# Attention steps placed in the middle of matmul groups, and x made with tokens on partitions for four of eight batches

## The chip, the cores and the metric

The kernel runs on one core of one Trainium2 chip. A core has a matrix engine (TensorE, PE in the profile, with PEld for its weight loads), three other compute engines (VectorE or DVE, ScalarE or ACT, GpSimd or POOL), a queue engine (SyncE or SP) that here only issues DMAs, and 16 DMA engines. TensorE writes into PSUM, which has eight banks of 128 partitions by 512 fp32 values. The metric is the device time of one execution in microseconds; lower is better.

## What is computed

Linear attention without softmax, an RMS norm over each head's 64 outputs, and then a bilinear feed-forward layer on the tokens.

```python
# q, k, v: (8 batches, 8 heads, 576 tokens, 64); g_norm: (64,)
kv = np.einsum('bhsd,bhse->bhde', k, v)
out = np.einsum('bhsd,bhde->bhse', q, kv)
rms = np.sqrt(np.mean(out * out, axis=-1, keepdims=True) + 1e-06)
attn = out / rms * g_norm
x = attn.transpose(0, 2, 1, 3).reshape(4608, 512)
# w_a, w_b: (512, 1536); w_out: (1536, 512)
result = ((x @ w_a) * (x @ w_b)) @ w_out
```

## The kernel before

**Tiles and stages.** The 4608 tokens are worked on in nine strips of 512 for the feed-forward layer, and in eight batches of 576 for the attention. Matrix operands are bf16. x is kept transposed, with its 512 features on partitions: four tiles `xt` of 128 features (two heads each, a "pair") by all 4608 tokens. A strip has 16 steps. Steps 0 to 11 are units (`ffn_ab`): eight matmuls of 512 columns, four with w_a (`part_a`), after which ACT copies the result to SBUF as bf16, and four with w_b (`part_b`), after which DVE multiplies the two into a tile `ab`. Steps 12 to 15 are outputs (`ffn_o`): twelve matmuls over the twelve `ab` tiles for 128 tokens, a copy to SBUF by DVE or ACT in turn, and a store.

**Banks.** Units rotate over banks 0, 1 and 2: unit n writes its two halves into banks 2n mod 3 and 2n+1 mod 3. So the first half of unit n uses the bank that DVE's multiply of unit n-2 frees. Outputs take bank 3 and, every second time, the next bank of the rotation. The attention steps use banks 4 and 5 for x, 6 and 7 for the sums of squares, and 7 for kv.

**Attention within the strips.** While strip s runs (1 to 6), batch s+1 is made: `slot(A, s, n)` is called after step n and issues what is due there. `kv` is 40 small matmuls and two copies into `kvb`, a block-diagonal tile of a pair's two 64x64 matrices. `x` of pair p is two matmuls of 288 columns that give x transposed; `psq` squares them on ACT; `pss` sums the squares over each head's 64 partitions by two matmuls with a block matrix of ones, followed by the reciprocal root on ACT; `pst` multiplies x by the root and by g on DVE, into `xt`. Before the change, kv is at step 5 in strips 1 and 2 and at step 2 later; x of the four pairs is at steps 7, 9, 11, 13 (4, 7, 10, 12 later), and pss and pst one step after each.

**Order.** There is no scheduler: each engine runs its instructions in the order in which the code issues them, with waits where one instruction needs another's result or its buffer. This holds for the DMA queues too. SP carries the stores of the outputs and the transposes of q (`transpose_q`, from a DRAM copy `qs` of a batch's q into `qT`). POOL carries the loads of later batches (`load_late`). `load_late(b)` starts with a one-element copy into `gate` that reads q's transposed tile of batch b-1 and so waits for its transpose, and then issues six DMAs (two for `qs`, two each for k and v). In strips from 2 on, `transpose_q(b+1)` and `load_late(b+2)` are issued after step 8.

**Start and end.** Batches 0 and 1 are made in other ways at the start, and are not touched by the change except for the name of `xt`. Strips 7 and 8 have no attention.

Of the kernel before, what the change touches and what calls it, by code (L numbers as in the profile page):

```python
# [8 lines left out]
FP32 = mybir.dt.float32  # L9
BF16 = mybir.dt.bfloat16  # L10
AF = mybir.ActivationFunctionType
# [4 lines left out]
def kernel(  # L16
# [11 lines left out]
    nc = tc.nc  # L28

    B, H, S, D = q.shape  # L30
    d_model = H * D
    n_tok = B * S
    d_ff = moe_w_a.shape[1]
    KC = d_model // 128
    FC = d_ff // 128
    NP = H // 2
    HF = S // 2
    STRIP = 512
# [2 lines left out]

    EC, EP = 6, 96
    EARLY = 2
    KORD = tuple(range(KC))

    pool = ctx.enter_context(tc.tile_pool(name="sb", bufs=1))
# [2 lines left out]
    def sb(shape, dt, name):  # L49
        return pool.tile(shape, dt, name=name, tag=name)  # L50
# [7 lines left out]

    kt = [sb([EP, H, EC, D], BF16, f"kt{i}") for i in range(EARLY)]
    vt = [sb([EP, H, EC, D], BF16, f"vt{i}") for i in range(EARLY)]  # L60

    LC = S // 128
    ktl = [sb([128, H, LC + 1, D], BF16, f"ktl{i}") for i in range(2)]
    vtl = [sb([128, H, LC + 1, D], BF16, f"vtl{i}") for i in range(2)]
    qt = [sb([EP, H, EC, D], BF16, f"qt{i}") for i in range(EARLY)]

# [1 line left out]
    kvs = [sb([128, NP, D], BF16, f"kvs{i}") for i in range(2)]  # L68

    kvb = [sb([128, NP, 128], BF16, f"kvb{i}") for i in range(2)]  # L70
    xt = [sb([128, n_tok], BF16, f"xt{i}") for i in range(KC)]
    abt = [[sb([128, STRIP], BF16, f"ab{i}_{f}") for f in range(FC)] for i in range(2)]
    a_sb = [sb([128, STRIP], BF16, f"asb{i}") for i in range(4)]
    sq = [sb([128, 2, HF], BF16, f"sq{i}") for i in range(3)]
    rs = [sb([128, 2, HF], FP32, f"rs{i}") for i in range(3)]
    o_sb = [sb([128, d_model], FP32, f"osb{i}") for i in range(4)]
    o_end = sb([128, d_model // 2], FP32, "o_end")
    ident = sb([128, 128], BF16, "ident")
# [3 lines left out]
    eps_t = sb([128, 1], FP32, "eps_t")  # L82
    warm = sb([128, 1], FP32, "warm")
    k32 = sb([EP, 2, EC, D], FP32, "k32")
    v32 = sb([EP, 2, EC, D], FP32, "v32")
    q32 = sb([EP, 2, EC, D], FP32, "q32")

    qc = sb([EP, EC, 2 * D], BF16, "qc")
    kc0 = sb([EP, EC, 2 * D], BF16, "kc0")
# [5 lines left out]
    P = psum.tile([128, 8, STRIP], FP32, name="P", tag="P")  # L95
    O = 3

    qs_d = {b: tc.dram_tile([S, d_model], BF16, name=f"qs{b}") for b in range(EARLY, B)}

# [23 lines left out]
    def load_late(b):  # L123
        if b > EARLY:

            nc.gpsimd.tensor_copy(gate, qT[(b - 1) % 2][0:1, 0, 0:1])  # L126
        d = qs_d[b].rearrange("t (h d) -> t h d", h=H)
        for hs in (slice(0, NP), slice(NP, H)):
            nc.gpsimd.dma_start(out=d[:, hs, :], in_=q[b, hs].rearrange("h t d -> t h d"))  # L129
        n = 128 * LC  # L130
        for t, src in ((ktl[b % 2], k), (vtl[b % 2], v)):
            nc.gpsimd.dma_start(
                out=t[:, :, 0:LC, :],
                in_=src[b, :, 0:n].rearrange("h (t c) d -> t h c d", c=LC),
            )
            nc.gpsimd.dma_start(
                out=t[0 : S - n, :, LC, :], in_=src[b, :, n:].rearrange("h t d -> t h d")
            )

    def transpose_q(b):  # L140
        nc.sync.dma_start_transpose(qT[b % 2], qs_d[b])


    class Attn:
# [5 lines left out]
        def kv(self, p, o):  # L150

            if self.b < EARLY:
                kk, vv, rows = kt[self.b], vt[self.b], [EP] * EC
# [66 lines left out]
        def pst(self, p, x0, hs=(0, 1)):  # L220
            for h in hs:
                t0 = self.b * S + h * HF
                nc.vector.scalar_tensor_tensor(  # L223
                    out=xt[p][:, t0 : t0 + HF],
                    in0=P[:, x0 + h, 0:HF],
                    scalar=g_col,
                    in1=rs[p % 3][:, h, :],
                    op0=ALU.mult,
                    op1=ALU.mult,
                )  # L230
# [10 lines left out]
                )  # L241


    class Unit:
        n = 0

# [5 lines left out]
        def mm(self, w, kcs):  # L252
            t0 = self.s * STRIP
            for kc in kcs:
                nc.tensor.matmul(  # L255
                    self.a if w is wa_t else self.b,
                    lhsT=w[:, kc, self.fc * 128 : (self.fc + 1) * 128],
                    rhs=xt[kc][:, t0 : t0 + STRIP],
                    start=(kc == KORD[0]),
                    stop=(kc == KORD[-1]),  # L260
                )
# [4 lines left out]

        def part_a(self, kcs=KORD):
            self.mm(wa_t, kcs)
            nc.scalar.copy(self.t, self.a)  # L269

        def part_b(self, kcs=KORD):
            self.mm(wb_t, kcs)
            nc.vector.tensor_mul(abt[self.s % 2][self.fc], self.b, self.t)  # L273

        def rest(self, kcs=KORD):
            self.part_a(kcs)
            self.part_b(kcs)

    n_ab = [0]

    def ffn_ab(s, fc):
        i = n_ab[0]
        n_ab[0] += 2
        Unit(s, fc, i % 3, (i + 1) % 3).rest()

    def store(t0, t, e0, e1, eng=nc.sync):
        i = 0
# [15 lines left out]
    def o_mm(s, g, i, fcs, e0=0, e1=d_model):  # L303
        for fc in fcs:
            nc.tensor.matmul(  # L305
                P[:, i, e0:e1],
                lhsT=abt[s % 2][fc][:, g * 128 : (g + 1) * 128],
                rhs=wo_t[:, fc, e0:e1],
                start=(fc == 0),
                stop=(fc == FC - 1),  # L310
            )

    def o_out(s, g, i):
        n = n_o[0]
        n_o[0] += 1
        t = o_sb[n % 4]
        if n % 2:
            nc.scalar.copy(t, P[:, i, :])  # L318
        else:
            nc.vector.tensor_copy(t, P[:, i, :])  # L320
        store(s * STRIP + g * 128, t, 0, d_model)

    def ffn_o(s, g, i=O):
        o_mm(s, g, i, range(FC))
        o_out(s, g, i)


# [41 lines left out]
    X, SS = (4, 0), 6  # L369


    A = Attn(0)
# [9 lines left out]
    t = P[:, 2, :].bitcast(BF16)[:, 0:S].rearrange("q (c t) -> q c t", c=EC)  # L382
# [4 lines left out]
    for c in range(EC):  # L387
        nc.tensor.matmul(
            P[:, SS, 0 : 2 * D],
            lhsT=kc0[:, c, :],  # L390
            rhs=vc[:, c, :],
            start=(c == 0),
            stop=(c == EC - 1),
# [10 lines left out]
    for p in range(1, NP):  # L404
        i = X[p % 2]
# [38 lines left out]
    for fc in range(4, FC):  # L444
        ffn_ab(0, fc)


    A = Attn(1)
    h1, h2 = range(0, FC // 2), range(FC // 2, FC)

    nc.sync.dma_start(out=gate_d, in_=vt[1][0:1, H - 1, EC - 1, D - 1 : D])
    ffn_o(0, 0, X[0])
    pieces = [(1, h1), (1, h2), (2, h1), (2, h2), (3, h1), (3, h2)]
    for n, (g, fcs) in enumerate(pieces):
# [24 lines left out]
    def slot(A, s, n):  # L479

        kb = P[:, 7, 0 : NP * D].rearrange("q (p e) -> q p e", e=D)
        k0, kn, xs = (5, 1, (7, 9, 11, 13)) if s < 3 else (2, 1, (4, 7, 10, 12))
        if k0 <= n < k0 + kn:
            for p in range((n - k0) * NP // kn, (n - k0 + 1) * NP // kn):
                A.kv(p, kb[:, p, :])
            if n == k0 + kn - 1:
                A.kv_out(slice(0, NP), kb)
        for p in range(NP):
            if n == xs[p]:
                A.x(p, X[0])  # L490
                A.psq(p, X[0])
            if n == xs[p] + 1:
                A.pss(p, SS)
                A.pst(p, X[0])

    for s in range(1, N_STRIP - 1):
        b = s + 1
        A = Attn(b) if b < B else None
        for n in range(FC + 4):
            if n >= FC:  # L500
                i = O if n % 2 == 0 else n_ab[0] % 3
                n_ab[0] += n % 2
                ffn_o(s, n - FC, i)
            elif s > 1 or n > 1:
                ffn_ab(s, n)
            if A:
                slot(A, s, n)
            if n == 8 and b + 1 < B:
                if s > 1:
                    transpose_q(b + 1)  # L510
                    if b + 2 < B:
                        load_late(b + 2)
                else:
                    load_late(3)
        if s == 1:
            transpose_q(3)
            load_late(4)
    last = N_STRIP - 1
    for fc in range(FC):
        ffn_ab(last, fc)  # L520
    for g in range(3):
        ffn_o(last, g, (O, 4)[g % 2])
# [38 lines left out]
```

## Time and profile before

| | |
|---|---|
| median of 8 runs | 322.63 us (322.34 to 323.46) |
| profiled execution | 322.58 us, of which the span from first to last instruction is 320.8 |
| granted TensorE clock | 1.000 |
| a strip (windows of TensorE's timeline, strips 4 and 5) | 33.9 us each |
| DVE and ACT busy in such a strip | 13.5 and 14.4 us |
| POOL's gate copies | 5, waiting 85.0 us in all |
| q transposes on SP | 6, 5.1 to 12.0 us from issue to landing |

A row of the groups names the line, the engine, the operation, what it writes and reads, its shape and count, then busy time in us and the mean of one in ns, then the idle time ahead of it and what ended it. A line of the timeline gives the start, the length, the engine, the line, the operation and the count, and in brackets the idle time before it. "POOL gate L126 <- DMA qT<-qs" in the waits means that the copy at L126 waited for that DMA, followed by total, number and longest. Matmuls are pipelined and their ends are modelled, so that the distance between starts tells more than the length.

### The profile page before, as it was taken

How to read it: one execution, taken by the hardware profiler on the slowest of the kernel's cores; microseconds unless marked ns; L12 is line 12 of the kernel's file. 1: busy time of each engine (PE TensorE's matmuls, PEld its weight loads, DVE VectorE, ACT ScalarE, POOL GpSimd, SP SyncE). 2: the span in 40 equal slices, each digit the busy share in tenths (PEclk: the TensorE clock that was granted, in tenths of full speed). 3: DMA queues.
4: the chain of work that ended last, by engine and by line, in shares of the span. 5: the costliest groups of instructions: out<-in, count | busy, mean ns of one | idle time of the engine just before them, and what ended most of it. 6: DMA issues, size and time to landing. Idle time of an engine off the chain costs nothing.

```text
span 320.8 us, 4732 instructions
## 1 busy us (share of the span) xinstructions
PE 315.2 (98%) x1883; PEld 150.7 (47%) x1883; DVE 124.8 (39%) x218; ACT 125.5 (39%) x217; POOL 70.3 (22%) x94
## 2 busy tenths in 40 slices
PE   8999999999999999999999999999999999999995
PEld 3444454444445444444444445444444444444443
DVE  4543344344234433453244423532354243313421
ACT  3643165353335423552355325432454233123310
POOL 8944990070034080160080000000000000000000
PEclk9999999999999999999999999999999999999999
DMA  8999999999369999999699151003000200020002
GB/s 180 197 196 200 197 181 232 138 95 158 88 90 150 144 117 209 101 125 163 141 72 151 65 116 25 0 35 99 0 2 0 98 35 0 24 90 21 0 33 98
DMA packets 79308, 32.60 MB, mean 102 GB/s; under 512 B 49974, under 2 KB 74806, under 8 KB 79286
## 3 DMA queue, kind: packets, MB, share of 16 engines
q0 software_dynamic: 59120, 18.44, 52.9%
q1 hardware_dynamic: 19810, 13.44, 17.9%
q10 hardware_dynamic: 356, 0.43, 0.4%
q8 instruction: 14, 0.23, 0.3%
q14 instruction: 8, 0.07, 0.1%
HBM read 37.75 MB, written 12.98 MB: 158 GB/s over the span
## 4 chain that ended last, share of the span: by engine, by line
PE 80%; DMA 13%; POOL 5%; issue 1%; ACT 0%; POOLq 0%
PE P L255 49%; PE P L305 26%; DMA wb_t<-in_moe_w_b_dram 5%; DMA vtl<-in_v_dram 5%; PE P L235 2%; PE P L209 2%; DMA kt<-in_k_dram 2%; DMA wo_t<-in_moe_w_out_dram 2%; PE P L158 1%; POOL qs L129 1%; POOL qt L106 1%; POOL wo_t L121 0%; POOL wa_t L360 0%; POOL wb_t L360 0%; POOL vt L106 0%
## 5 line engine op out<-in xcount | busy, mean ns | idle before, releaser
L273 DVE TENSOR_TENSOR ab<-P,asb 128x512 bf16<-128x512 f32 x108 | 74.5, 692 | 124.6 <-PE P L255 123.6
L255 PE MATMUL P<-xt,wa_t 128*128 128x512 bf16 x432 | 111.9, 379 | 0.0
L255 PE MATMUL P<-xt,wb_t 128*128 128x512 bf16 x432 | 111.7, 379 | 0.0
L305 PE MATMUL P<-wo_t,ab 128*128 128x512 bf16 (+1 forms) x444 | 97.9, 373 | 0.0
L269 ACT CAST asb<-P 128x512 bf16<-128x512 f32 x108 | 63.0, 585 | 81.8 <-PE P L255 80.3
L255 PEld LDWEIGHTS <-wb_t 128*128 128x128 bf16 x432 | 42.2, 98 | 50.9
L305 PEld LDWEIGHTS <-ab 128*128 128x128 bf16 x444 | 43.1, 98 | 45.6
L255 PEld LDWEIGHTS <-wa_t 128*128 128x128 bf16 x432 | 41.7, 98 | 44.8 <-issue 0.5
L223 DVE SCALAR_TENSOR_TENSOR xt<-P,g_col,rs 128x288 bf16<-128x288 f32 x64 | 30.1, 513 | 24.3 <-ACT rs L213 24.3
L213 ACT ACTIVATE rs<-P,eps_t 128x576 f32<-128x576 f32 (+1 forms) x33 | 23.9, 727 | 20.8 <-PE P L209 16.5
L318 ACT COPY osb<-P 128x512 f32<-128x512 f32 x17 | 10.0, 585 | 48.6 <-PE P L305 46.8
L205 ACT ACTIVATE sq<-P 128x576 bf16<-128x576 f32 x31 | 20.2, 650 | 20.6 <-PE P L235 18.3
L320 DVE COPY osb<-P 128x512 f32<-128x512 f32 x18 | 12.5, 692 | 32.4 <-PE P L305 32.3
L129 POOL DMA_DIRECT2D qs<-in_q_dram x12 | 19.6, 1636 | 2.2 <-issue 2.1
L126 POOL COPY gate<-qT 1x1 bf16<-1x1 bf16 x5 | 0.9, 176 | 85.0 <-DMA qT<-qs 85.0
L209 PE MATMUL P<-sq,ones 128*128 128x288 bf16 x64 | 13.2, 286 | 0.5 <-ACT sq L205 0.4
L235 PE MATMUL P<-qT,kvb 128*128 128x288 bf16 x56 | 11.9, 286 | 0.0
L169 ACT CAST kvb<-P 64x256 bf16<-64x256 f32 (+1 forms) x20 | 6.0, 301 | 11.8 <-PE P L158 11.7
L209 PEld LDWEIGHTS <-ones 128*128 128x128 bf16 x64 | 6.2, 98 | 7.4 <-issue 0.4
L330 PE MATMUL P<-zeros 128*128 128x512 bf16 x17 | 7.2, 569 | 1.2 <-DVE eps_t L345 1.2
L235 PEld LDWEIGHTS <-kvb 128*128 128x128 bf16 x56 | 5.5, 98 | 6.0
L121 POOL DMA_DIRECT2D wo_t<-in_moe_w_out_dram x12 | 6.4, 531 | 6.7 <-DMA wb_t<-in_moe_w_b_dram 3.3
(55 smaller groups left out, 83.5 us busy)
## 6 DMA issues: line engine op xcount, KB each, us to landing
out_dram<-osb SPq DMA_DIRECT2D x23, 256.0 KB, 2.0
qs<-in_q_dram POOLq DMA_DIRECT2D x12, 288.0 KB, 6.1
ktl<-in_k_dram POOLq DMA_DIRECT2D x6, 512.0 KB, 8.5
vtl<-in_v_dram POOLq DMA_DIRECT2D x6, 512.0 KB, 10.6
out_dram<-osb SPq DMA_DIRECT2D x13, 128.0 KB, 2.3
wo_t<-in_moe_w_out_dram POOLq DMA_DIRECT2D x12, 128.0 KB, 5.9
wa_t<-in_moe_w_a_dram POOLq DMA_DIRECT2D x5, 256.0 KB, 9.0
wb_t<-in_moe_w_b_dram POOLq DMA_DIRECT2D x5, 256.0 KB, 9.6
```

What stands on the lines that cost most here:

```text
L129: nc.gpsimd.dma_start(out=d[:, hs, :], in_=q[b, hs].rearrange("h t d -> t h d"))
L205: nc.scalar.activation(sq[p % 3], P[:, i0 : i0 + 2, 0:HF], AF.Square)
L209: nc.tensor.matmul(P[:, i0 + h, 0:HF], lhsT=ones, rhs=sq[p % 3][:, h, :], start=True, stop=True)
L213: nc.scalar.activation(rs[p % 3][:, h0:h1, :], P[:, i0 + h0 : i0 + h1, 0:HF], AF.Abs_reciprocal_sqrt, bias=eps_t,)
L223: nc.vector.scalar_tensor_tensor(out=xt[p][:, t0 : t0 + HF], in0=P[:, x0 + h, 0:HF], scalar=g_col, in1=rs[p % 3][:, h, :], op0=ALU.mult, o ...
L235: nc.tensor.matmul(P[:, i0 + h, 0:HF], lhsT=kvb[self.b % 2][:, p, :], rhs=self.qT[:, p, h * HF : (h + 1) * HF], start=True, stop=True,)
L255: nc.tensor.matmul(self.a if w is wa_t else self.b, lhsT=w[:, kc, self.fc * 128 : (self.fc + 1) * 128], rhs=xt[kc][:, t0 : t0 + STRIP], st ...
L269: nc.scalar.copy(self.t, self.a)
L273: nc.vector.tensor_mul(abt[self.s % 2][self.fc], self.b, self.t)
L305: nc.tensor.matmul(P[:, i, e0:e1], lhsT=abt[s % 2][fc][:, g * 128 : (g + 1) * 128], rhs=wo_t[:, fc, e0:e1], start=(fc == 0), stop=(fc == F ...
L318: nc.scalar.copy(t, P[:, i, :])
L320: nc.vector.tensor_copy(t, P[:, i, :])
```

## The change

Three things are changed.

First, `slot` may be called in the middle of a step too: between `part_a` and `part_b` of a unit and between the two halves of an output's twelve matmuls, with n less a half. For batches 2 and 3 (strips 1 and 2), kv goes from step 5 to 6, x of the pairs to 7, 9.5, 12 and 13.5, and pss with pst to 8, 10.5, 12.5 and 14.

Second, for batches 4 to 7 (strips 3 to 6), x is made with tokens on partitions. The 576 tokens are five chunks (four of 128, one of 64), and a chunk starts with every step from 3.5 on. `tx` is four matmuls of 128 columns with the chunk of q as weights and `kvb` as moving operand, into one of the banks 4, 5, 6, and a Square on ACT from PSUM into `sqt` (fp32). `tss`, half a step later, sums each head's 64 squares on DVE. `trs`, half a step later, takes the reciprocal root on ACT (8 values a token) and multiplies it with g on POOL into `sqt`, 512 values a token. `txt`, half a step later, multiplies that with x in PSUM on DVE, into a bf16 tile `x_tok` (three buffers, in the place of the first q tile), and SP issues a DMA transpose from there into `xt`. pss with its 288-column matmuls and pst fall away for these batches. The last multiply of chunk 4 is issued at step 8.5, its product at 9.

Third, `xt` becomes one tile with the four groups of features in its middle dimension, and g is loaded once more, onto all 128 partitions, by SP.

The lines that set the order of step 8 are not changed: `transpose_q(b+1)` and `load_late(b+2)` come after `slot(A, s, 8)`.

```diff
+    def tx(self, c, i):
+        t0 = c * 128
+        n = min(128, S - t0)
+        for p in range(NP):
+            nc.tensor.matmul(
+                P[0:n, i, p * 128 : (p + 1) * 128],
+                lhsT=self.qT[:, p, t0 : t0 + n],
+                rhs=kvb[self.b % 2][:, p, :], start=True, stop=True,
+            )
+        nc.scalar.activation(
+            sqt[c % 2][0:n], P[0:n, i, :].rearrange("t (h d) -> t h d", h=H), AF.Square
+        )
+    def tss(self, c):
+        n = min(128, S - c * 128)
+        nc.vector.reduce_sum(sst[c % 2][0:n], sqt[c % 2][0:n], axis=mybir.AxisListType.X)
+    def trs(self, c):
+        n = min(128, S - c * 128)
+        nc.scalar.activation(
+            rst[c % 2][0:n], sst[c % 2][0:n],
+            AF.Abs_reciprocal_sqrt, bias=eps_t[0:n], scale=1.0 / D,
+        )
+        nc.gpsimd.tensor_mul(
+            sqt[c % 2][0:n],
+            rst[c % 2][0:n].unsqueeze(2).to_broadcast([n, H, D]),
+            g_all[0:n].unsqueeze(1).to_broadcast([n, H, D]),
+        )
+    def txt(self, c, i):
+        t0 = c * 128
+        n = min(128, S - t0)
+        t = x_tok[:, c % 3]
+        nc.vector.tensor_mul(
+            t[0:n], P[0:n, i, :].rearrange("t (h d) -> t h d", h=H), sqt[c % 2][0:n]
+        )
+        t0 += self.b * S
+        nc.sync.dma_start_transpose(
+            xt[:, :, t0 : t0 + n], t[0:n].rearrange("t h d -> t (h d)")
+        )
...
-    def ffn_ab(s, fc):
+    def ffn_ab(s, fc, between=None):
         i = n_ab[0]
         n_ab[0] += 2
-        Unit(s, fc, i % 3, (i + 1) % 3).rest()
+        u = Unit(s, fc, i % 3, (i + 1) % 3)
+        u.part_a()
+        if between:
+            between()
+        u.part_b()
...
-    def ffn_o(s, g, i=O):
-        o_mm(s, g, i, range(FC))
+    def ffn_o(s, g, i=O, between=None):
+        o_mm(s, g, i, range(FC // 2))
+        if between:
+            between()
+        o_mm(s, g, i, range(FC // 2, FC))
         o_out(s, g, i)
...
     def slot(A, s, n):
-        k0, kn, xs = (5, 1, (7, 9, 11, 13)) if s < 3 else (2, 1, (4, 7, 10, 12))
...
+        if s < 3:
+            k0, xs, ss = 6, (7, 9.5, 12, 13.5), (8, 10.5, 12.5, 14)
+        else:
+            k0, xs, ss = 2, (4, 7, 10, 12), (5, 8, 11, 13)
+        if n == k0:
+            for p in range(NP):
+                A.kv(p, kb[:, p, :])
+            A.kv_out(slice(0, NP), kb)
+        if A.b >= BY_TOKEN:
+            for c in range(LC + 1):
+                d = n - (k0 + 1.5) - c
+                i = 4 + c % 3
+                if d == 0:
+                    A.tx(c, i)
+                elif d == 0.5:
+                    A.tss(c)
+                elif d == 1:
+                    A.trs(c)
+                elif d == 1.5:
+                    A.txt(c, i)
+            return
+        if n in xs:
+            p = xs.index(n)
+            A.x(p, X[0])
+            A.psq(p, X[0])
+        if n in ss:
+            p = ss.index(n)
+            A.pss(p, SS)
+            A.pst(p, X[0])
...
         for n in range(FC + 4):
+            amid = (lambda n=n: slot(A, s, n - 0.5)) if A else None
             if n >= FC:
                 i = O if n % 2 == 0 else n_ab[0] % 3
                 n_ab[0] += n % 2
-                ffn_o(s, n - FC, i)
+                ffn_o(s, n - FC, i, amid)
             elif s > 1 or n > 1:
-                ffn_ab(s, n)
+                ffn_ab(s, n, amid)
             if A:
                 slot(A, s, n)
             if n == 8 and b + 1 < B:
                 if s > 1:
                     transpose_q(b + 1)
                     if b + 2 < B:
                         load_late(b + 2)
```

More of the change, by code (lines that the diff above doesn't have):

```diff
@@ L43 @@
     EARLY = 2
+    BY_TOKEN = 4
     KORD = tuple(range(KC))
@@ L70 @@
     kvb = [sb([128, NP, 128], BF16, f"kvb{i}") for i in range(2)]
-    xt = [sb([128, n_tok], BF16, f"xt{i}") for i in range(KC)]
+    xt = sb([128, KC, n_tok], BF16, "xt")
     abt = [[sb([128, STRIP], BF16, f"ab{i}_{f}") for f in range(FC)] for i in range(2)]
@@ L75 @@
     rs = [sb([128, 2, HF], FP32, f"rs{i}") for i in range(3)]
+    sqt = [sb([128, H, D], FP32, f"sqt{i}") for i in range(2)]
+    sst = [sb([128, H], FP32, f"sst{i}") for i in range(2)]
+    rst = [sb([128, H], FP32, f"rst{i}") for i in range(2)]
+    g_all = sb([128, D], FP32, "g_all")
     o_sb = [sb([128, d_model], FP32, f"osb{i}") for i in range(4)]
@@ L85 @@
     v32 = sb([EP, 2, EC, D], FP32, "v32")
-    q32 = sb([EP, 2, EC, D], FP32, "q32")
+    q_x = sb([128, 2 * EC * D], FP32, "q_x")
+    q32 = q_x[0:EP].rearrange("p (h c d) -> p h c d", h=2, c=EC)
+    x_tok = q_x.bitcast(BF16).rearrange("p (c h d) -> p c h d", c=3, h=H)
     qc = sb([EP, EC, 2 * D], BF16, "qc")
@@ L223, in pst @@
                 nc.vector.scalar_tensor_tensor(
-                    out=xt[p][:, t0 : t0 + HF],
+                    out=xt[:, p, t0 : t0 + HF],
                     in0=P[:, x0 + h, 0:HF],
@@ L241, in x @@
                 )
+        def tx(self, c, i):
[5 more added lines that the diff above has]
+                    lhsT=self.qT[:, p, t0 : t0 + n],
+                    rhs=kvb[self.b % 2][:, p, :],
+                    start=True,
+                    stop=True,
+                )
[8 more added lines that the diff above has]
+            nc.scalar.activation(
+                rst[c % 2][0:n],
+                sst[c % 2][0:n],
+                AF.Abs_reciprocal_sqrt,
+                bias=eps_t[0:n],
+                scale=1.0 / D,
+            )
[15 more added lines that the diff above has]
+            )
     class Unit:
@@ L257, in mm @@
                     lhsT=w[:, kc, self.fc * 128 : (self.fc + 1) * 128],
-                    rhs=xt[kc][:, t0 : t0 + STRIP],
+                    rhs=xt[:, kc, t0 : t0 + STRIP],
                     start=(kc == KORD[0]),
@@ L445 @@
         ffn_ab(0, fc)
+    nc.sync.dma_start(out=g_all, in_=g_norm.partition_broadcast(128))
     A = Attn(1)
@@ L481, in slot @@
         kb = P[:, 7, 0 : NP * D].rearrange("q (p e) -> q p e", e=D)
-        k0, kn, xs = (5, 1, (7, 9, 11, 13)) if s < 3 else (2, 1, (4, 7, 10, 12))
-        if k0 <= n < k0 + kn:
-            for p in range((n - k0) * NP // kn, (n - k0 + 1) * NP // kn):
-                A.kv(p, kb[:, p, :])
[L486 to L494, printed above, removed]
+        if s < 3:
[4 more added lines that the diff above has]
+            for p in range(NP):
+                A.kv(p, kb[:, p, :])
+            A.kv_out(slice(0, NP), kb)
[20 more added lines that the diff above has]
+            A.pst(p, X[0])
     for s in range(1, N_STRIP - 1):
```

## The prediction

> **What bounds the kernel now.** I read the page first, then the table of groups, then TensorE's timeline strip by strip, then the timelines of POOL and of SP.
>
> From the page:
>
> ```profile
> PE 315.2 (98%) x1883; PEld 150.7 (47%) x1883; DVE 124.8 (39%) x218; ACT 125.5 (39%) x217; POOL 70.3 (22%) x94
> ...
> PE 80%; DMA 13%; POOL 5%; issue 1%; ACT 0%; POOLq 0%
> ```
>
> TensorE is busy almost throughout and carries the chain that ended last. So a TensorE instruction saved is time saved, and a TensorE stall is time lost, one for one.
>
> TensorE's timeline (start us, length, engine, line, operation, count, idle before it), pieces of four places:
>
> ```profile
> 7.28 0.50 PE L388 MATMUL P<-vc,kc 96*128 96x128 bf16 x6
> ...
> 61.06 0.32 PE L158 MATMUL P<-vtl,ktl 128*64 128x64 bf16 x8
> 61.91 0.69 PE L158 MATMUL P<-vtl,ktl 128*64 128x64 bf16 x32 [0.54 <-DMA vtl<-in_v_dram]
> ...
> 69.95 0.53 PE L235 MATMUL P<-qT,kvb 128*128 128x288 bf16 x2
> 70.31 1.02 PE L255 MATMUL P<-xt,wa_t 128*128 128x512 bf16 x4
> ...
> 162.99 0.41 PE L235 MATMUL P<-qT,kvb 128*128 128x288 bf16 x2
> 163.24 1.03 PE L255 MATMUL P<-xt,wa_t 128*128 128x512 bf16 x4
> 164.10 1.03 PE L255 MATMUL P<-xt,wb_t 128*128 128x512 bf16 x4
> ```
>
> Ends are modelled, so I price by the distance of starts. Four 512-column matmuls take 164.10 - 163.24 = 0.86 us, 0.216 each; a unit (eight) takes 1.73, an output (twelve) 2.59. Two 288-column ones take 163.24 - 162.99 = 0.25, about 0.12 each. At 69.95 the same pair takes 0.36: 0.12 us of waiting for the banks. Six 128-column matmuls start within 0.50 - 0.22 = 0.28 us, 0.057 each. In strip 1, kv waits 0.54 us for vtl. Strips 3 to 6 have no stall of TensorE.
>
> The two element-wise rows that free the units' banks (mean ns of one after the busy time):
>
> ```profile
> L273 DVE TENSOR_TENSOR ab<-P,asb 128x512 bf16<-128x512 f32 x108 | 74.5, 692 | 124.6 <-PE P L255 123.6
> ...
> L269 ACT CAST asb<-P 128x512 bf16<-128x512 f32 x108 | 63.0, 585 | 81.8 <-PE P L255 80.3
> ```
>
> POOL's timeline in strip 3, SP's timeline, and one line of the waits:
>
> ```profile
> 134.64 0.18 POOL L126 COPY gate<-qT 1x1 bf16<-1x1 bf16 x1 [14.21 <-DMA qT<-qs]
> 135.13 3.26 POOL L129 DMA_DIRECT2D qs<-in_q_dram  x2 [0.31 <-issue]
> 138.37 0.91 POOL L132 DMA_DIRECT2D ktl<-in_k_dram  x1
> 139.26 0.70 POOL L136 DMA_DIRECT2D ktl<-in_k_dram  x1
> 139.94 0.91 POOL L132 DMA_DIRECT2D vtl<-in_v_dram  x1
> 140.81 0.72 POOL L136 DMA_DIRECT2D vtl<-in_v_dram  x1
> ```
>
> ```profile
> 123.70 7.12 SPq L141 DMA_TRANSPOSE qT<-qs  x1
> ...
> 154.83 2.23 SPq L141 DMA_TRANSPOSE qT<-qs  x1
> ...
> 188.72 3.11 SPq L141 DMA_TRANSPOSE qT<-qs  x1
> ```
>
> ```profile
> POOL gate L126 <- DMA qT<-qs: 85.0, 5, 22.5
> ```
>
> POOL runs in order. The gate copy holds it until the transposed q has landed (22.5 us at the longest), and the six loads behind it occupy POOL from 134.64 to 141.53, 6.9 us. Before the change nobody waits for POOL there. From the transpose's issue at 154.83 to its gate (160.92 in the same timeline) it is 6.1 us; landings are 5.1 to 12.0 us, the long ones while loads run.
>
> **What the Trainium skill says.** "GPSIMD Engine Reference", section 3.1, gives 4497 ns for a two-input fp32 tensor_tensor of 2048 elements a lane, so 1.12 us for 512; with about 0.1 us of start (POOL's smallest memset, at L545, takes 0.10) I estimate 1.2 us. No trace of before has such an operation. "DMA: Bandwidth & Descriptors", section DMA Transpose (X-bar), says that transposes are issued from SP or ACT alone; here all six stand on SP, so the new ones share its queue with the stores and q's transpose. "TensorE: Matmul & The Clock Gate", Part 1, says that after an idle window of 3.4 us the array runs at half rate until it has been busy for such a window. The trace agrees at the start: the 512-column dummies follow each other at 0.43 us (weight loads at 4.16 and 4.59) until about 7 us, then at full rate. It shows no idle stretch later.
>
> **Part 1: batches 2 and 3, finer places.** Same instructions, other places. kv comes one unit later (1.73 us), which covers its 0.54 us wait. x now comes 1.5 steps after the last pss, at least 2.6 us, where the trace needs 104.08 + 0.12 - 102.11 = 2.1; four waits of 0.12 go. Gain 0.54 + 0.48 = 1.0 us. Pair 3 still ends at step 14, so strip 2's start is no later. If vtl should be later still, at most the 0.54 stays.
>
> **Part 2: batches 4 to 7, TensorE.** Out: 8 x and 8 pss, 16 x 0.12 = 1.96 us. In: 20 matmuls of 128 columns, 20 x 0.057 = 1.14. Gain 0.82 a batch, 3.3 over four. Both parts: 4.3.
>
> **Part 2: the loop of one chunk.** Each chunk passes ACT (Square, about 0.60 by L269), DVE (sum of 512 from SBUF, no such row: between the 0.56 of the cast of 768 from SBUF at L377 and the 0.69 of L273, I take 0.60), ACT (rsqrt of 8 columns, 0.21 by the 0.20 of the one-column activation at L347), POOL (1.2), DVE (product, 0.69 by L273). In DVE's queue they alternate: ab, product of c, sum of c+1, next ab. Product of c waits for POOL, POOL for rsqrt, rsqrt for the sum of c, and the sum of c stands behind the product of c-1. So one round is 0.60 + 0.21 + 1.2 + 0.69 + four handovers (0.17) = 2.87 us, while TensorE brings a unit with a chunk every 1.73 + 0.23 = 1.96. Counted from a strip's start (unit 4 ends at 9.83, after kv):
>
> - products end at 13.7, 16.6, 19.4, 22.3 for chunks 0 to 3;
> - ab of units 7, 8, 9 stand behind them: 17.9, 20.7, 23.6;
> - a unit's first half needs the bank that ab of two units before frees, so unit 10 starts at 20.8 and not 19.6, unit 11 waits for 23.6, and ends at 25.4. Without waits it ends at 22.8.
>
> Behind DVE's waiting product stand the ab and through them TensorE; behind ACT's waiting rsqrt the next Square and copy. Loss 2.5 us in each strip from 3 to 6. Bounds: with POOL at 0.8 us the round is 2.5 and the loss 1.1; at 2.0, 5.7. I see no reason for a gain here.
>
> **Part 2: chunk 4 behind the gate.** The queues' order in the changed program: on SP, x transposes of chunks 0 to 3, then q's transpose of batch b+1, then chunk 4's. On POOL, the multiplies of chunks 0 to 3, then gate and six loads of batch b+2, then the multiply of chunk 4. That holds in strips 3 and 4 (batches 4 and 5); in 5 and 6 there is no load. Before, q's transpose issued as soon as the previous strip's stores were out; now it comes after product 3: 22.3 + 0.6 (its x transpose, estimated from 2.23 us for 576 rows) = 22.9. Gate at +6.1 = 29.0 (the loads are over by then, so not the long landing), POOL free at +6.9 = 35.9, multiply to 37.1, product to 37.8, ab of unit 10 to 38.5, of 11 to 39.2. TensorE runs on through unit 11 and ten matmuls of the first output, to 27.5, and then has nothing: 11 us idle. The output ends at 39.5, against 25.4 without any wait: 14.1 us lost in each of the two strips (the 2.5 of the loop is within it). With POOL at 0.8 and a landing of 5.1 it is 11.2; with POOL at 2.0, 18.1.
>
> An idle of 11 us is more than three such windows, so TensorE comes back at half rate for 3.4 to 6.8 us: 1.7 to 3.4 us lost, I take 2.5, twice 5.0; at the low end 0, since no later stretch shows it.
>
> x itself is late for nobody: the next strip first needs chunks 0 and 1 at most, which are out by 17. The loads of b+2 come later, but have a strip to spare. The merge of x^T into one tile adds no wait within a strip. g's load of 128 rows is small and off the path.
>
> **Sum.** The profiled execution took 322.58 us (span 320.8 plus 1.8 around it), the median is 322.63. 322.6 - 4.3 + 2 x 14.1 + 2 x 2.5 + 5.0 = 356.5.
>
> **Rivals.**
> - B, the gate alone: POOL is quick (0.65 us), the loop costs 0.6 a strip, the gate 11.6. 318.3 + 24.4 + 5.0 = 347.7. For it: POOL's small operations are quick here. Against: none has two fp32 inputs of this size.
> - C, a slow loop: POOL needs 2.0 us with its broadcast operands. 318.3 + 2 x 18.1 + 2 x 5.7 + 5.0 = 370.9.
> - D, faster: TensorE has 5.6 us of other work after the place of the last product (two units and ten matmuls, 3.45 + 2.16). If q's transpose and the loads held POOL for less than that, and the multiply took under 0.5 us, all waits would be hidden and the saved matmuls alone counted: 318.3. It decides below 5.6 us; against it stand 5.1 (the quickest landing) + 6.9 measured.
> - The x transposes could themselves be late, so that strip 4's first unit waits for them; with twenty microseconds to spare I give that no time of its own.
>
> **How the numbers follow.** The likeliest case 0.60, B 0.19, C 0.12, D 0.06, all cancelling 0.03. Differences under 0.2% (0.65 us) can't be told from none here. Predicted 356.5. The low end is POOL at 0.8, landing 5.1, no cold clock: 318.3 + 2 x 11.2 + 2 x 1.1 = 342.9; the high end stops just short of C's centre. Range 343 to 370; it holds most of the first case, B, and a part of C. Faster 0.06, same 0.03, slower 0.91.
>
> **What would show it.** In strips 3 and 4, DVE's product of chunk 4 waits over 10 us for POOL, POOL's gate follows the q transpose that was issued after chunk 3's, and TensorE stands idle in the first output, then runs 512 columns at 0.43 us. In strips 5 and 6 the products are about 2.9 us apart and TensorE loses 2 to 3 us. Strips 1 and 2 have no stall in x or kv. I am wrong if TensorE has no idle stretch over 5 us in strip 3, or if the products keep pace with the units.

## The result

The changed kernel takes 353.35 us (median of 11 runs, 352.5 to 357.55) against 322.6 us before: a ratio of 1.097, with a 95% interval from 1.095 to 1.100. The profiled execution took 356.11 us, with a span of 354.3 us and a mean granted clock of 0.957. The forecast was 356.5 us, in a range of 343 to 370, and slower.

From the page of the kernel after (busy time by engine, the row of the granted clock in 40 slices of the span, and the chain that ended last):

```profile
PE 320.7 (91%) x1899; PEld 149.5 (42%) x1899; DVE 133.0 (38%) x226; ACT 117.1 (33%) x225; POOL 91.1 (26%) x114
...
PEclk9699999999999999957999959999999999999999
...
PE 78%; POOL 6%; DMA 5%; issue 4%; DVE 4%; ACT 1%; DVEq 0%; SPq 0%; POOLq 0%
```

TensorE's share of the span fell from 98% to 91%. DVE has come into the chain with 4%, and of POOL's share, 6% where it was 5%, half is now the new multiply (`sqt` at L282, 3% in the page's list by lines). The clock row has three dips that were not there before: one near the start and two in the middle.

I read the start of every strip's first unit from TensorE's timeline; the differences are the strips' lengths in us. The last two columns belong to experiments further down.

| strip | before | after | loads after chunk 4 | product later, g late |
|---|---|---|---|---|
| before strip 1 | 50.61 | 53.53 | 51.98 | 50.57 |
| 1 and 2 | 68.99 | 67.79 | 67.80 | 67.79 |
| 3 | 33.90 | 48.56 | 35.08 | 33.28 |
| 4 | 33.90 | 48.30 | 35.15 | 33.28 |
| 5 | 33.90 | 35.14 | 35.15 | 33.28 |
| 6 | 33.89 | 35.16 | 35.15 | 33.28 |

Of the 33.5 us by which the span grew, 29.1 are in strips 3 and 4, 2.5 in strips 5 and 6, and 2.9 ahead of strip 1; strips 1 and 2 gained 1.2.

TensorE's timeline of strip 3 after the change:

```profile
141.57 1.02 PE L312 MATMUL P<-xt,wa_t 128*128 128x512 bf16 x4 [0.62 <-DVE ab L330]
...
144.33 1.02 PE L312 MATMUL P<-xt,wa_t 128*128 128x512 bf16 x4 [0.88 <-DVE ab L330]
...
146.05 2.32 PE L366 MATMUL P<-wo_t,ab 128*128 128x512 bf16 x10
158.69 11.35 PE L366 MATMUL P<-wo_t,ab 128*128 128x512 bf16 x38 [10.32 <-DVE ab L330]
169.88 1.03 PE L312 MATMUL P<-xt,wa_t 128*128 128x512 bf16 x4
```

Units 10 and 11 begin late, because DVE has not freed their banks. Then ten matmuls of the first output run, and TensorE waits 10.32 us for the `ab` of unit 10. The 38 matmuls after that take 169.88 - 158.69 = 11.19 us, where 38 x 0.216 = 8.21 are due at the pace of TensorE alone.

DVE's timeline of the same strip shows what `ab` of unit 10 (L330) stood behind:

```profile
136.86 0.69 DVE L292 TENSOR_TENSOR q_x<-P,sqt 128x512 bf16<-128x512 f32 x1 [0.89 <-POOL sqt L282]
137.47 0.68 DVE L271 TENSOR_REDUCE sst<-sqt 128x8 f32<-128x512 f32 x1
138.06 0.68 DVE L330 TENSOR_TENSOR ab<-P,asb 128x512 bf16<-128x512 f32 x1
139.63 0.69 DVE L292 TENSOR_TENSOR q_x<-P,sqt 128x512 bf16<-128x512 f32 x1 [0.89 <-POOL sqt L282]
...
143.60 0.67 DVE L330 TENSOR_TENSOR ab<-P,asb 128x512 bf16<-128x512 f32 x1
157.36 0.68 DVE L292 TENSOR_TENSOR q_x<-P,sqt 64x512 bf16<-64x512 f32 x1 [13.08 <-POOL sqt L282]
157.97 1.27 DVE L330 TENSOR_TENSOR ab<-P,asb 128x512 bf16<-128x512 f32 x2
```

Two products (L292) of neighbouring chunks are 139.63 - 136.86 = 2.77 us apart, each after 0.89 us of waiting for POOL: this is the loop. The product of chunk 4 waits 13.08 us, and the two `ab` of units 10 and 11 run right behind it.

POOL's timeline, and then SP's, show why:

```profile
141.33 1.04 POOL L282 TENSOR_TENSOR sqt<-rst,g_all 128x512 f32<-128x512 f32 x1 [1.73 <-ACT rst L275]
149.30 0.18 POOL L136 COPY gate<-qT 1x1 bf16<-1x1 bf16 x1 [6.93 <-DMA qT<-qs]
149.79 3.30 POOL L139 DMA_DIRECT2D qs<-in_q_dram  x2 [0.31 <-issue]
...
155.53 0.73 POOL L146 DMA_DIRECT2D vtl<-in_v_dram  x1
156.23 1.10 POOL L282 TENSOR_TENSOR sqt<-rst,g_all 64x512 f32<-64x512 f32 x1
```

```profile
134.81 9.51 SPq L296 DMA_TRANSPOSE xt<-q_x  x4
144.49 2.59 SPq L151 DMA_TRANSPOSE qT<-qs  x1
158.07 1.17 SPq L296 DMA_TRANSPOSE xt<-q_x  x1
```

SP issues q's transpose at 144.49, after the fourth x transpose. POOL's gate waits for it until 149.30, the six loads occupy POOL until 156.23, and only then does the multiply of chunk 4 run. POOL would have been free for it from 142.4, and its sum (L271, at 143.01) was ready at 143.7, the root behind it at 144.0.

### The profile page after: what moved, and what is told of

Its sections match the earlier page's. It is cut to its first block, busy times and chain, and to the rows that moved or that the text cites. A ratio compares the mean times of both kernels' runs of the same rounds, so it can differ in the third digit from the quotient of the medians.

```text
span 354.3 us, 4883 instructions
## 1 busy us (share of the span) xinstructions
PE 320.7 (91%) x1899; PEld 149.5 (42%) x1899; DVE 133.0 (38%) x226; ACT 117.1 (33%) x225; POOL 91.1 (26%) x114
## 4 chain that ended last, share of the span: by engine, by line
PE 78%; POOL 6%; DMA 5%; issue 4%; DVE 4%; ACT 1%; DVEq 0%; SPq 0%; POOLq 0%
PE P L312 45%; PE P L366 27%; POOL sqt L282 3%; DMA qT<-qs 3%; DVE sst L271 2%; DMA vt<-in_v_dram 2%; PE P L168 2%; PE P L219 1%; DVE ab L330 1%; PE P L245 1%; PE P L258 1%; POOL qs L139 1%; ACT rst L275 1%; PE P L192 1%; DMA xt<-q_x 1%
## 5 line engine op out<-in xcount | busy, mean ns | idle before, releaser
L366 PE MATMUL P<-wo_t,ab 128*128 128x512 bf16 (+1 forms) x444 | 102.7, 387 | 20.8 <-DVE ab L330 20.8
L330 DVE TENSOR_TENSOR ab<-P,asb 128x512 bf16<-128x512 f32 x108 | 73.8, 688 | 102.7 <-PE P L312 94.9
L282 POOL TENSOR_TENSOR sqt<-rst,g_all 128x512 f32<-128x512 f32 (+1 forms) x20 | 20.9, 1046 | 106.3 <-ACT rst L275 106.3
L292 DVE TENSOR_TENSOR q_x<-P,sqt 128x512 bf16<-128x512 f32 (+1 forms) x20 | 13.8, 690 | 39.6 <-POOL sqt L282 39.5
L233 DVE SCALAR_TENSOR_TENSOR xt<-P,g_col,rs 128x288 bf16<-128x288 f32 x32 | 15.0, 512 | 14.6 <-ACT rs L223 14.6
L223 ACT ACTIVATE rs<-P,eps_t 128x576 f32<-128x576 f32 (+1 forms) x17 | 12.0, 713 | 9.9 <-PE P L219 9.9
L215 ACT ACTIVATE sq<-P 128x576 bf16<-128x576 f32 x15 | 9.7, 650 | 11.8 <-PE P L245 8.5
L271 DVE TENSOR_REDUCE sst<-sqt 128x8 f32<-128x512 f32 (+1 forms) x20 | 13.5, 674 | 0.0
L275 ACT ACTIVATE rst<-sst,eps_t 128x8 f32<-128x8 f32 (+1 forms) x20 | 6.0, 301 | 21.2 <-DVE sst L271 21.2
L265 ACT ACTIVATE sqt<-P 128x512 f32<-128x512 f32 (+1 forms) x20 | 11.6, 581 | 0.0
L258 PEld LDWEIGHTS <-qT 128*128 128x128 bf16 (+1 forms) x80 | 5.9, 100 | 5.5 <-issue 1.7
## 6 DMA issues: line engine op xcount, KB each, us to landing
vtl<-in_v_dram POOLq DMA_DIRECT2D x6, 512.0 KB, 10.5
```

The lines of the kernel that those rows point to most:

```text
L223: nc.scalar.activation(rs[p % 3][:, h0:h1, :], P[:, i0 + h0 : i0 + h1, 0:HF], AF.Abs_reciprocal_sqrt, bias=eps_t,)
L233: nc.vector.scalar_tensor_tensor(out=xt[:, p, t0 : t0 + HF], in0=P[:, x0 + h, 0:HF], scalar=g_col, in1=rs[p % 3][:, h, :], op0=ALU.mult, o ...
L265: nc.scalar.activation(sqt[c % 2][0:n], P[0:n, i, :].rearrange("t (h d) -> t h d", h=H), AF.Square)
L271: nc.vector.reduce_sum(sst[c % 2][0:n], sqt[c % 2][0:n], axis=mybir.AxisListType.X)
L282: nc.gpsimd.tensor_mul(sqt[c % 2][0:n], rst[c % 2][0:n].unsqueeze(2).to_broadcast([n, H, D]), g_all[0:n].unsqueeze(1).to_broadcast([n, H, D]),
L292: nc.vector.tensor_mul(t[0:n], P[0:n, i, :].rearrange("t (h d) -> t h d", h=H), sqt[c % 2][0:n])
```

## The experiments

**The loads after chunk 4's multiply.** If POOL's order is the cause, one moved call is enough.

```diff
-                    if b + 2 < B:
+                    if b + 2 < B and s < 3:
                         load_late(b + 2)
...
+            if n == 9 and s >= 3 and b + 2 < B:
+                load_late(b + 2)
```

> In strips 3 and 4 the loads of batch b+2 with their gate are issued after chunk 4's multiply (step 9) and not before it (step 8); nothing else differs from the changed kernel (353.35 us). My theory (POOL's queue holds chunk 4's multiply behind gate and loads): the 10.3 us idle of TensorE in the first output of strips 3 and 4 goes, and with it about 3.0 us of half-rate matmuls after each; what stays is the loop's loss of about 2 us in each of strips 3 to 6. 353.35 - 2 x 13.3 = 326.8 us. Rival, the token-wise work itself is what costs (DVE, ACT and POOL can't keep pace, the gate only coincides): no change beyond 2 us, 351 to 353. Rival, the x transposes on SP's queue and the DMA engines cost: no change either.

Measured: 327.85 us (4 runs), ratio 1.019 [1.012, 1.026]. TensorE's timeline at the same place:

```profile
144.50 10.52 PE L366 MATMUL P<-wo_t,ab 128*128 128x512 bf16 x48
154.86 1.03 PE L312 MATMUL P<-xt,wa_t 128*128 128x512 bf16 x4
```

All 48 matmuls of the four outputs run without a break. Strips 3 and 4 are 13.5 and 13.2 us shorter, strips 5 and 6 unchanged. So the multiply's place behind gate and loads carries most of the loss, 25.5 us in the medians, with nothing of the token-wise work taken away. What is left, 35.15 us a strip against 33.90 before, I put down to the loop; the product half a step later, below, tests that.

**q's transpose first.** This splits the hold on POOL into its two parts.

```diff
+            if n == 2 and s >= 3 and b + 1 < B:
+                transpose_q(b + 1)
             if n == 8 and b + 1 < B:
                 if s > 1:
-                    transpose_q(b + 1)
+                    if s < 3:
+                        transpose_q(b + 1)
```

> In strips 3 and later q's transpose of batch b+1 is issued at step 2, ahead of the x transposes on SP; the loads with their gate stay at step 8, ahead of chunk 4's multiply. My theory: the gate opens at once, and POOL is held by the six issues alone (6.95 us): the multiply of chunk 4 starts 6.9 us sooner, TensorE's idle shrinks from 10.3 to about 3.5 us in strips 3 and 4, and the half rate after it is shorter or gone: 353.35 - 13.8 - (0 to 6) = 333.5 to 339.5 us. If the wait for the DMA transpose were not part of it: 353. If the loads' issue were not part of it, and the gate all: 327, as without the loads ahead.

Measured: 337.03 us (4 runs), ratio 1.045 [1.042, 1.048]. POOL's timeline in strip 3:

```profile
139.89 1.04 POOL L282 TENSOR_TENSOR sqt<-rst,g_all 128x512 f32<-128x512 f32 x1 [1.73 <-ACT rst L275]
140.88 0.18 POOL L136 COPY gate<-qT 1x1 bf16<-1x1 bf16 x1
140.99 3.30 POOL L139 DMA_DIRECT2D qs<-in_q_dram  x2
...
147.44 1.09 POOL L282 TENSOR_TENSOR sqt<-rst,g_all 64x512 f32<-64x512 f32 x1
```

The median lies within the 333.5 to 339.5 that I expected. The gate no longer waits; the loads still hold POOL from 140.88 to 147.44. TensorE's idle in strip 3 is then 2.96 us and not 10.32. Both parts are real: the wait for the transpose costs about 7 us a strip in idle, the issue of the loads the rest.

**TensorE kept busy in the idle stretch.** Forty matmuls of zeros, whose result nobody reads, stand before the last two matmuls of the first output of strips 3 and 4.

```diff
+        if between and s in (3, 4) and g == 0:
+            o_mm(s, g, i, range(FC // 2, FC - 2))
+            dummy(40, 6)
+            o_mm(s, g, i, range(FC - 2, FC))
```

> The changed kernel with 40 matmuls of zeros (8.6 us at full rate) into a free bank before the last two matmuls of the first output of strips 3 and 4, where TensorE is idle for 10.3 us; their result is not used. My theory (the idle makes TensorE come back at half rate, 3.0 us lost each time): TensorE comes back at full rate, 353.35 - 6.0 = 347.3 us, with the wait for POOL unchanged. If the slow matmuls after the idle have another cause: 353.

Measured: 351.14 us (4 runs, 349.29 to 352.19), ratio 1.088 [1.084, 1.092]. In the profiled execution:

```profile
146.55 8.80 PE L399 MATMUL P<-zeros 128*128 128x512 bf16 x40
156.81 0.39 PE L366 MATMUL P<-wo_t,ab 128*128 128x512 bf16 x1 [1.46 <-DVE ab L330]
157.41 8.16 PE L366 MATMUL P<-wo_t,ab 128*128 128x512 bf16 x37 [0.21 <-DVE ab L330]
165.40 1.03 PE L312 MATMUL P<-xt,wa_t 128*128 128x512 bf16 x4
```

The last 37 matmuls take 165.40 - 157.41 = 7.99 us, 0.216 each: full rate. The second of the 38 starts 0.60 us after the first, because the `ab` of unit 11 comes only then. So at full rate the 38 take 165.40 - 156.81 = 8.59 us and not 8.21, and what half rate costs has to be counted from 8.59. The windows view of the changed kernel right after its idle stretch shows the other case (stretch, its length, busy time and instructions of PE, PEld, DVE, ACT and POOL, then the granted clock, the DMA share and GB/s):

```profile
158.69:162.00 3.31, 3.31 (x8) 1.14 (x9) 1.24 (x2) 0.00 (x0) 0.00 (x0) 0.50 1.57 192
162.00:166.00 4.00, 4.00 (x15) 1.49 (x13) 0.00 (x0) 0.58 (x1) 0.00 (x0) 0.68 0.96 148
166.00:169.88 3.88, 3.88 (x19) 1.75 (x18) 0.69 (x1) 0.00 (x0) 0.00 (x0) 1.00 0.49 139
```

Half the clock, then full. Between the profiled executions strips 3 and 4 became 2.8 and 2.3 us shorter, but the medians differ by only 2.2 us in all, less than half of what I expected. The executions of this kernel had clocks from 0.990 to 1.0, those of the changed kernel from 0.952 to 0.971, so something else varied too; a later pair takes it out.

**The new places alone.** Batches 4 to 7 go back to the old way.

```diff
-    BY_TOKEN = 4
+    BY_TOKEN = 8
```

> The first part alone: batches 2 and 3 at the new places in the middle of steps, batches 4 to 7 made as before the change but with the finer slot function and the one x tile. My theory: no wait of kv or x in strips 1 and 2, 322.6 - 1.0 = 321.6 us. Rival, the mid-unit places hurt somewhere (ACT's order, a bank): above 323.

Measured: 322.8 us (12 runs), ratio 1.0026 [1.0001, 1.0051]. The expected 1.0 us of gain is not there. Strips 1 and 2 did become 1.2 us shorter, and no kv or x waits in them; but strip 1 began at 52.00 and not at 50.61. From the view of DMA issues of this kernel, first 10 us (last number: median us to landing):

```profile
qt<-in_q_dram POOLq DMA_DIRECT2D x3, 144.0 KB, 6.9
kt<-in_k_dram POOLq DMA_DIRECT2D x3, 144.0 KB, 7.0
vt<-in_v_dram POOLq DMA_DIRECT2D x3, 144.0 KB, 6.7
...
g_all<-in_g_norm_dram SPq DMA_DIRECT2D x1, 32.0 KB, 5.8
```

Before the change the first three landed after 5.7, 5.8 and 5.9 us; the first of them there:

```profile
qt<-in_q_dram POOLq DMA_DIRECT2D x3, 144.0 KB, 5.7
```

TensorE now waits 0.74 us for pair 1's q:

```profile
8.24 0.45 PE L192 MATMUL P<-ident,qt 96*64 96x96 bf16 x12 [0.74 <-DMA qt<-in_q_dram]
```

g's load has nothing to wait for in SP's queue, so it goes out at 1.7 us, although the code issues it after strip 0's units. That it delays the others is only likely so far; the next run moves it alone.

**g's load late.** The same, with that load behind the wait for batch 1's last load.

```diff
-    nc.sync.dma_start(out=g_all, in_=g_norm.partition_broadcast(128))
...
     nc.sync.dma_start(out=gate_d, in_=vt[1][0:1, H - 1, EC - 1, D - 1 : D])
+    nc.sync.dma_start(out=g_all, in_=g_norm.partition_broadcast(128))
```

> The new places alone, with g's load to 128 partitions issued behind the wait for the last of batch 1's loads (about 46 us) and not at the start. Strips 1 and 2 took 1.2 us less with the new places, but strip 1 began 1.4 us later. Theory A: g's load, 128 packets on the queues at 1.7 us, delays the first loads of q, k and v (landing 6.9 instead of 5.7 us) and so the start: 322.8 - 1.4 = 321.4 us. Theory B: the one x tile or the shared q tile delays the start: 322.8.

Measured: 321.5 us (7 runs), ratio 0.9965 [0.9951, 0.9978]; strip 1 begins at 50.83, and the three loads land after 5.6, 5.7 and 5.5 us again. Theory A: the single `xt` and the shared q tile cost nothing that shows. (The page counts 144 packets more than before the change, not 128.)

**The changed kernel with g late, and with zeros on top.** The pair that settles the price of the half rate.

> The changed kernel with g's load issued behind the wait for batch 1's loads, nothing else. Theory (g's early load delays the first loads, and the longer start lets TensorE fall to half rate in some executions): 353.35 - 1.4 = 352.0 us or somewhat less, and less spread than the 352.5 to 357.6 of the changed kernel. Rival, the spread comes from the idle stretches in strips 3 and 4: the same spread.

> As e10_after_g_late, with 46 matmuls of zeros (9.9 us) in the idle stretches of strips 3 and 4. In the profiled executions with 40 of them the two strips were 2.8 and 2.3 us shorter than in the changed kernel, yet the medians only 2.2 us apart in all. Theory (half rate after each idle stretch costs 2.5 to 3.0 us each time): 5 to 6 us below e10_after_g_late, about 346.5 us. Rival (it costs about 1 us each in most executions): 2 us below, 350.

Measured: 352.56 us (5 runs, 351.81 to 353.39), ratio 1.094 [1.092, 1.096], with the load alone moved; 348.86 us (4 runs, 348.73 to 349.31), ratio 1.083 [1.081, 1.084], with 46 matmuls of zeros as well. TensorE's timeline of strip 3 without the zeros:

```profile
155.85 10.44 PE L366 MATMUL P<-wo_t,ab 128*128 128x512 bf16 x38 [10.28 <-DVE ab L330]
166.12 1.03 PE L312 MATMUL P<-xt,wa_t 128*128 128x512 bf16 x4
```

The 38 matmuls after the idle take 166.12 - 155.85 = 10.27 us, and 10.29 in strip 4: 1.7 us over the 8.59 that they take with the zeros. In the profile of the changed kernel itself it was 11.19 - 8.59 = 2.6 in strip 3 and 10.70 - 8.59 = 2.1 in strip 4. The medians differ by 3.7 us, 1.85 a stretch, below the theory's 2.5 and above the rival's 1. So the half rate is worth about 1.7 to 2.6 us after each stretch, and differs from execution to execution.

The spread of the changed kernel is gone with g's early load. Five runs would be few to say so, but the other versions agree: 9 of 46 executions with g's load early lie 1.3 us or more above the median of their version, and none of 24 with it late.

**The product half a step later.** On top of the loads after chunk 4's multiply, this takes the sum of the next chunk out from behind the waiting product. A third buffer for `sqt` is needed; it takes the place of the first k tile.

```diff
-                elif d == 1.5:
+                elif d == 2:
                     A.txt(c, i)
```

> The loads of batch b+2 after chunk 4's multiply, as in the run before, and each chunk's product half a step later (2 steps after tx, not 1.5), with a third sqt buffer. The sum of chunk c+1 then stands ahead of the product of chunk c in DVE's queue, and POOL has time to finish. My theory (the loop sum - rsqrt - POOL - product - next sum takes 2.77 us against a unit's 1.95): the products no longer wait, and the 2 us of each of strips 3 to 6 go: 322.8 (places alone, same start) - 3.3 (fewer matmul columns) = 319.5 us. Rival, DVE itself is too slow for sum, product and ab in one unit (0.67 + 0.69 + 0.69 = 2.05 us against 1.95): about 0.1 us a chunk stays, 320. Rival, the loss of e1_load_after has another source: 327.9.

> As e5_product_later, with g's load issued late. Theory A: 319.5 - 1.4 = 318.1 us. Theory B: 319.5.

Measured: 320.62 us (10 runs), ratio 0.995 [0.993, 0.996], and with g late 319.31 us (4 runs), ratio 0.990 [0.988, 0.992]. DVE's timeline of the latter in strip 3:

```profile
130.30 0.69 DVE L332 TENSOR_TENSOR ab<-P,asb 128x512 bf16<-128x512 f32 x1 [0.66 <-PE P L314]
130.91 0.68 DVE L273 TENSOR_REDUCE sst<-sqt 128x8 f32<-128x512 f32 x1
131.50 0.68 DVE L294 TENSOR_TENSOR q_x<-P,sqt 128x512 bf16<-128x512 f32 x1
132.25 0.69 DVE L332 TENSOR_TENSOR ab<-P,asb 128x512 bf16<-128x512 f32 x1
```

The three operations of a unit now fill DVE without a wait for POOL, 132.25 - 130.30 = 1.95 us a round, TensorE's own pace. Each of strips 3 to 6 takes 33.28 us, 1.8 to 1.9 less than with the loads moved alone: that was the loop. Both runs are 1.1 to 1.2 us above what I expected. Some 0.8 of it comes from the fewer columns, which gained less than worked out (at 133.07 one of four matmuls is missing from the record); the rest stays open:

```profile
132.84 0.39 PE L260 MATMUL P<-kvb,qT 128*128 128x128 bf16 x4
133.07 1.03 PE L314 MATMUL P<-xt,wb_t 128*128 128x512 bf16 x3
133.93 1.03 PE L314 MATMUL P<-xt,wa_t 128*128 128x512 bf16 x4
134.89 0.41 PE L260 MATMUL P<-kvb,qT 128*64 128x128 bf16 x4
135.23 1.04 PE L314 MATMUL P<-xt,wb_t 128*128 128x512 bf16 x4
```

A chunk of 128 tokens takes 133.07 - 132.84 = 0.23 us, as priced. The chunk of 64 tokens, whose weights are 64 wide, starts 0.10 us after its turn (133.93 + 0.86 = 134.79), and the next group starts 0.34 us later: together 0.21 us more, a quarter of the gain of the strip. TensorE's weight loads show where it begins:

```profile
132.63 0.42 PEld L260 LDWEIGHTS <-qT 128*128 128x128 bf16 x4
...
134.88 0.25 PEld L260 LDWEIGHTS <-qT 128*64 128x64 bf16 x4 [0.42 <-issue]
135.23 0.55 PEld L314 LDWEIGHTS <-wb_t 128*128 128x128 bf16 x4
```

In the chunk of 128 the weight loads begin at 132.63, 0.21 us ahead of their matmuls. The narrow ones begin together with theirs (134.88 and 134.89), and so do the wide ones that follow them (both 135.23). kv's matmuls, also with weights 64 wide, are 0.10 us late too in the kernel before (124.88, where 123.92 + 0.86 = 124.78 was their turn). That the change of width is the cause is likely from this, but no run varies the width alone.

**Batches 2 and 3 by token too.** As the last, with BY_TOKEN at 2 and the loads of batch 5 after strip 2.

> As e8_product_later_g_late, with batches 2 and 3 made with tokens on partitions too, and the loads of batch 5 issued after strip 2. 0.8 us less of matmuls in each of strips 1 and 2: 318.1 - 1.6 = 316.5 us, if POOL is free there when the chunks come (the loads of batch 3, issued at step 8 ahead of the first multiply at 8.5, must have left POOL by then). If they have not, a wait of up to 5 us in strip 1: 321.

Measured: 318.65 us (4 runs), ratio 0.988 [0.986, 0.990]. This is the fastest version, about 4 us below the kernel before, but 2.1 us above the expectation. About 1.2 of these come with the version that it starts from. Strip 2 took 33.28 us like the others; strip 1 took 34.08, more than the 33.90 with x made the old way. POOL's timeline there:

```profile
70.36 0.72 POOL L148 DMA_DIRECT2D vtl<-in_v_dram  x1
71.06 2.09 POOL L284 TENSOR_TENSOR sqt<-rst,g_all 128x512 f32<-128x512 f32 x2
```

The loads of batch 3 held POOL until 71.06, and the first two multiplies ran one behind the other after them. Chunk 3's tx then waited 0.64 us for a product. It is the same conflict as in strips 3 and 4, in small: 0.64 us and not the up to 5 that I had allowed for.

## Why the prediction was right, step by step

- **TensorE bounds, stalls count one for one:** held. Strip 3 takes 48.56 - 33.28 = 15.28 us more than without the waits (last column of the table). That is the sum of what TensorE waited between starts (0.78 and 1.04 for units 10 and 11, 10.48 in the first output) and of the 2.98 by which the 38 matmuls exceed 8.21: 0.38 due to the second `ab`, 2.60 to the half rate.
- **The new places, -1.0 us:** the mechanism held, strips 1 and 2 gave 1.2 us.
- **"g's load of 128 rows is small and off the path":** wrong. It is small, but it lands among the first loads: 1.4 us at the start with the new places alone, and 2.9 in the profiled execution of the changed kernel, where TensorE's clock dipped there too (0.50 from 12 to 14 us). This cancels the gain of the places.
- **Fewer columns, -0.82 us a batch:** 0.62. The term was priced as 20 equal matmuls; the four with 64-wide weights, with the start behind them, cost 0.21 us more.
- **The loop, 2.5 us a strip:** 1.8 to 1.9. The round was 2.77 us for the forecast 2.87. The mis-sized terms are POOL's multiply, 1.04 us and not 1.2, and the handovers, 0.07 and not 0.17; the sum (0.67) and the root (0.30) took more than assumed (0.60 and 0.21), and part of the error cancelled.
- **Chunk 4 behind gate and loads, 14.1 us with the loop in it:** 48.56 - 33.28 - 2.60 = 12.7 us in strip 3, 12.9 in strip 4. Its parts: product 3 ended 21.8 us into the strip (forecast 22.3); its x transpose took SP 1.19 us (0.6, worked out by the rows); q's transpose to gate took 4.8 us (6.1, taken from a strip in which stores had just gone out); the loads held POOL for 6.9 (6.9); TensorE was idle for 10.3 and 10.5 us (11).
- **Half rate afterwards, 2.5 us each:** 2.6 and 2.1 in the profiled execution, 1.7 in that with g late.
- **Sum:** the gate was over-sized by 2.6 us over both strips, the loop by 1.3 over the other two and the half rate by 0.3; the columns' gain was 0.8 too large, and the start was missed, 2.9 us in the profiled execution. The mechanism is what held. That the sizes cancel to 0.4 us in that execution (356.11 for 356.5) is luck; the median is 3 us lower. Of the rivals, B (a quick POOL, the loop at 0.6 us a strip) and C (a POOL at 2.0 us) fell by the round of 2.77 us, with POOL at 1.04. D, all waits hidden, is what the kernel becomes with three small moves: 319.3 us, where I had put it at 318.3.

## What to carry to other kernels

Before giving an engine a place in a chain that has a deadline, write down what stands ahead of that instruction in its queue: here one multiply of 1 us stood behind a wait for a DMA and seven microseconds of load issue, and issuing the loads one step later, behind the multiply, was worth 25 us. When two engines alternate in a loop, put the next round's independent work ahead of the operation that waits. And a DMA with nothing to wait for goes out when its queue reaches it, not where the code places it, so a small load can still fall among the first loads.

## What the runs showed of the hardware that was not expected

- A 32 KB load that repeats one row of 256 bytes onto 128 partitions, issued at 1.7 us, put off the landings of the loads beside it: 6.7 to 7.0 us, against 5.5 to 5.7 with that load late.
- After matmuls with 128-wide weights, a group of four 128-column matmuls with 64-wide weights starts 0.10 us late, and the group behind it starts 0.34 us after it, against 0.23 with 128-wide weights.
- Three microseconds of idle are enough for the half rate at one time and not at another: in the profiled execution with q's transpose first, 37 matmuls ran at full rate (158.49 - 150.50 = 7.99 us) after 2.96 us of idle in strip 3, and took 198.83 - 189.15 = 9.68 us after the same idle in strip 4, with a granted clock of 0.55 at first (189.15 to 192.00).
- An x transpose of 128 by 512 from SBUF to SBUF took SP 1.19 us to issue, a little under half of what q's transpose of 576 rows took (2.59); chunk 4's, with 64 rows, still took 1.17.
- The clock column of the profile misses a half rate: in the kernel before it reads 1.00 from 0 to 7 us, where weight loads for 512-column matmuls follow each other at 0.43 us (4.16 and 4.59).
